# Range test of w1 as one minimum on VectorE, key and query bits' copies on ScalarE, in a fused hash-attention and Fourier-mixing kernel

## The chip, the cores and the metric

The kernel runs on one core of a Trainium2 chip. The metric is the device time of one execution in microseconds, as the median of several runs.

## The reference

The inputs are q, k and v of shape (4, 8, 768, 64), a projection of shape (64, 6), and two weight matrices that arrive as 64-bit floats. What is computed, cut to what matters:

```python
# attention: a query sees only the keys of its own hash bucket
q_bits = (einsum('bhsd,dk->bhsk', q, proj) > 0); k_bits = (same with k)
mask = bucket(q_bits)[..., :, None] == bucket(k_bits)[..., None, :]
scores = where(mask, (q @ k.T) / 8, -1e9)
attn = softmax(scores); x = attn @ v          # then heads side by side: (4, 768, 512)
# Fourier mixing and a two-layer network
u = x + real(fft2(x))
un = (u - mean(u)) / sqrt(var(u) + 1e-6)
out = u + relu(un @ w1) @ w2                  # w1 (512, 2048), w2 (2048, 512)
```

## The kernel before

The work goes by batch (4) and, inside a batch, by pair of heads (4), so there are 16 pairs, numbered 0 to 15. Each pair is handled in 6 chunks of 128 keys. For a chunk, TensorE makes the scores (L909), ScalarE takes their exp (L922, two halves, one for each half of the queries), VectorE adds the result to a running sum (L1043), and TensorE multiplies with v (L947). The bucket mask is, in pairs 0 to 4, a second product that is added to the scores in the same bank (L898): bits of the queries times bits of the keys, scaled so that a mismatch drives the exponent far down. From pair 5 the mask is a comparison on VectorE (L936).

The function `prepare(n + 1)` is a generator that is advanced once for each chunk of pair n. It transposes q and k of the next pair (L779 on VectorE), takes the squares' sums (L761 on ScalarE), makes the hash products (L812 on TensorE) and thresholds them (L816 on VectorE, reading the product's bank). For the query, two multiplications (L822) then make two masked copies of the bits; for the key, four copies (L828) put the bits at the partitions of the other half. These run after chunks 3 and 4. In pair 0 the key's copies alternate between VectorE and ScalarE (`evac`, L535 and L537).

During batch 0 a second generator, `weights1`, brings in w1. It is advanced in four of five chunks. Each of its 16 steps takes a block of 128x512 64-bit words that has been loaded into one of seven raw buffers, and `narrow` turns them into 32-bit floats: shifts and masks of the high words (L639, L643), a conversion of the low words on ScalarE (L647), an integer addition (L649). Then `narrow` tests the range: Abs of the high words (L654) and a Relu of `least` minus that with an accumulated sum (L655), whose sum is above zero where a magnitude was too small for a 32-bit float. The sum goes to a column of `strange`, which at the end, by a maximum (L1627), selects a slow path that is never taken with these inputs. `fetch` reloads the raw buffer (L704) when its last reader is done. After four steps the column means of w1 are made (`average`: ws at L664, part at L669, wm at L672) and subtracted (`centre`, L678). w2 passes through the same `narrow` later (its addition is L652).

At the end of a pair, `scale` normalises: key sums (L957), transposes and reciprocals (L979, L981, L982), small copies (L990), a transpose (L995) and a multiplication (L999). The last pair of a batch starts the Fourier stage's first folds (L1124 to L1142).

The buffers that matter here: the scores have two banks (`ps_sc`), and a chunk uses both, so scores of the next chunk start when the exp of the first half has read its bank. The exp's results have two buffers (`pks`), so the exp of chunk c+2 waits for the addition of chunk c to the running sum. `ps_1` has two banks for bits, ws and sums.

Batch 0 is written inside `manual_schedule`: each engine executes its instructions in the order in which the program issues them. One chunk's order is: scores and exp, addition to the sum, the previous pair's scaling, values of the previous chunk, a step of `prepare`, a step of `weights1`. From batch 1 on, a scheduler orders the engines.

Of the kernel before, what the change touches and what calls it, by code (L numbers as in the profile page):

```python
# [11 lines left out]
F32 = mybir.dt.float32  # L12
BF16 = mybir.dt.bfloat16
I32 = mybir.dt.int32
I64 = mybir.dt.int64
U32 = mybir.dt.uint32
AF = mybir.ActivationFunctionType
ALU = mybir.AluOpType
AX = mybir.AxisListType
# [5 lines left out]
DFF = 4 * DM  # L25
# [5 lines left out]
NDC = DM // P  # L31
GTT = 2
GT = GTT * P
WC = 512
# [451 lines left out]
def _main(  # L486
# [13 lines left out]
    nc = tc.nc  # L500
# [13 lines left out]
    def wt(shape, dtype, tag, name, bufs=2):  # L514
        return work.tile(shape, dtype, tag=tag, name=name, bufs=bufs)
# [78 lines left out]
    own = const.tile([P, 2], F32, tag="own", name="own")  # L594
# [25 lines left out]
    w2 = const.tile([P, NFC, DM], F32, tag="w2", name="w2")  # L620


    least = const.tile([P, 1], F32, tag="least", name="least")
    nc.gpsimd.memset(least, float(897 << 20))
    strange = const.tile([P, 2 * NDC * DFF // WC], F32, tag="strange", name="strange")
    nc.gpsimd.memset(strange, 0.0)

    def narrow(dst, raw, col, low=None):


        lo, hi = (raw[..., i] for i in range(2))
        t = lo.bitcast(F32)
        if low is None:

            low, t = lo, hi.bitcast(F32)
        di = dst.bitcast(I32)


        nc.vector.tensor_scalar(  # L639
            di, hi, 3, (1 << 30) - 1,  # L640
            op0=ALU.logical_shift_left, op1=ALU.bitwise_and,
        )
        nc.vector.scalar_tensor_tensor(  # L643
            di, hi, -(1 << 30), di, op0=ALU.bitwise_and, op1=ALU.bitwise_or
        )

        nc.scalar.activation(low, lo.bitcast(U32), AF.Copy, scale=2.0**-29)  # L647
        if len(di.shape) == 2:
            nc.vector.tensor_tensor(di, di, low, op=ALU.add)  # L649
        else:  # L650
            for i in range(di.shape[1]):
                nc.vector.tensor_tensor(di[:, i], di[:, i], low[:, i], op=ALU.add)  # L652

        nc.scalar.activation(t, hi, AF.Abs)  # L654
        nc.scalar.activation(  # L655
            t, t, AF.Relu, bias=least, scale=-1.0, accum_out=strange[:, col : col + 1]
        )
# [108 lines left out]
    def prepare(n):  # L766

        lite = n in LITE
        ts = {}
        for io, nm in enumerate("qk"):  # L770
            tn = nat.pop((nm, n))
            tt = wt([P, S], F32, nm + "t", f"{nm}t{n}")
            if n > 0:
                to, at = tt, tn
                if nm == "q":

                    to = tt.rearrange("p (i r n) -> p r i n", i=2, r=2)
                    at = tn.rearrange("p (r i n) -> p r i n", i=2, r=2)
                nc.vector.transpose(to, at)  # L779
            for g in range(2) if n == 0 else ():  # L780
                ps = pt([P, 3, P], f"tr{nm}{n}_{g}")
                for i in range(3):
                    c = 2 * i + g if nm == "q" else 3 * g + i
                    nc.tensor.transpose(ps[:, i, :], tn[:, c * P : (c + 1) * P], ident)
                if nm == "q":
                    for i in range(2):
                        dst = tt[:, i * HALF + g * HALF // 2 : i * HALF + (g + 1) * HALF // 2]
                        evac(
                            dst.rearrange("p (j c) -> p c j", c=3),
                            ps[:, :, i * D : (i + 1) * D],  # L790
                        )
                else:
                    evac(
                        tt[:, g * HALF : (g + 1) * HALF],
                        ps.rearrange("p c t -> p (c t)"),
                    )
            ts[nm] = tt
            yield
            norm(n, io, tn)
        if lite:  # L800

            qk = wt([P, 2, S], BF16, "qb", f"qkb{n}")
            qz = qk[:, 0].rearrange("p (g s) -> p g s", g=2)
            bits = {"q": qz[:, 0], "k": qk[:, 1, 0:HALF]}
            for io, nm in enumerate("qk"):
                ps = pt([P, HALF], f"bits{nm}{n}")
                for j in range(4):  # L810
                    h, g = divmod(j, 2)
                    nc.tensor.matmul(  # L812
                        ps[32 * j : 32 * j + 32, :], pjw[:, h * D : h * D + 32],
                        ts[nm][:, g * HALF : (g + 1) * HALF], start=True, stop=True,
                    )
                nc.vector.tensor_scalar(  # L816
                    bits[nm], ps, 0.0, off[:, io : io + 1],
                    op0=ALU.is_gt, op1=ALU.subtract,
                )
                if io == 0:  # L820
                    for g in (1, 0):
                        nc.vector.tensor_scalar(  # L822
                            qz[:, g], qz[:, 0], own[:, g : g + 1], None, op0=ALU.mult
                        )
                else:
                    for j in range(4):
                        to, at = (slice(32 * i, 32 * i + 32) for i in (j, j ^ 1))
                        (evac if n == 0 else nc.vector.tensor_copy)(  # L828
                            qk[to, 1, HALF:S], qk[at, 1, 0:HALF]
                        )  # L830
                yield
            preps[n] = ts["q"], ts["k"], qk, None
            return

        ps = pt([P, HALF], f"bits{n}")
        for j in range(4):
            src = ts["qk"[j // 2]][:, (j % 2) * HALF : (j % 2 + 1) * HALF]
            nc.tensor.matmul(  # L838
                ps[32 * j : 32 * j + 32, :], pj, src, start=True, stop=True
            )  # L840
        bt = wt([P, HALF], BF16, "bt", f"bt{n}")
        nc.vector.tensor_scalar(bt, ps, 0.0, None, op0=ALU.is_gt)
        yield

        qb = wt([P, 2, S], BF16, "qb", f"qb{n}")
        kb = wt([P, 2, NT], F32, "kb", f"kb{n}")
        for h in range(2):
            ps = ps_sc.tile([P, 2, 512], F32, tag="sc", name=f"qb{n}_{h}")
            for g in range(2):
                rows = slice(32 * g, 32 * g + 32)  # L850
                with behind() if g + h else nullcontext():
                    last[0] = nc.tensor.matmul(
                        ps[:, g, 0:HALF], pw[rows, h, :], bt[rows, :],
                        start=True, stop=True,
                    )
            evac(qb[:, h, :].rearrange("p (g s) -> p g s", g=2), ps[:, :, 0:HALF])
        ps = ps_sc.tile([P, 2, 512], F32, tag="sc", name=f"kb{n}")
        for c in range(NT):
            g, i = divmod(c, NT // 2)
            rows = slice(64 + 32 * g, 96 + 32 * g)  # L860
            with behind() if c else nullcontext():
                last[0] = nc.tensor.matmul(
                    ps[:, g, 2 * i : 2 * i + 2], bt[rows, i * P : (i + 1) * P],
                    pw[rows, :, 0], start=True, stop=True,
                )
        nc.vector.tensor_copy(
            kb.rearrange("p h (g i) -> p g i h", g=2),
            ps[:, :, 0:NT].rearrange("p g (i h) -> p g i h", h=2),
        )
        preps[n] = ts["q"], ts["k"], qb, kb  # L870
# [731 lines left out]
    for b in range(B):  # L1602
# [17 lines left out]
        if b == B - 1:  # L1620
            roomy[0] = True

            ms = const.tile([P, 3], F32, tag="ms", name="ms")
            nc.vector.tensor_reduce(ms[:, 0:2], norms, axis=AX.X, op=ALU.max)
            nc.vector.tensor_reduce(ms[:, 2:3], strange, axis=AX.X, op=ALU.max)  # L1627
            ps = pt([1, 3, P], "norms_t")
            for io in range(3):
                nc.tensor.transpose(ps[:, io, :], ms[:, io : io + 1], ident)  # L1630
            mt = const.tile([1, 5], F32, tag="mt", name="mt")
            nc.vector.tensor_reduce(mt[:, 0:3], ps, axis=AX.X, op=ALU.max)
            nc.vector.tensor_tensor(mt[:, 3:4], mt[:, 0:1], mt[:, 1:2], op=ALU.mult)
            nc.vector.tensor_scalar(
                mt[:, 4:5], mt[:, 3:4], (SAFE / SCALE / 2) ** 2, None, op0=ALU.is_gt
            )
            fl = const.tile([1, 1], I32, tag="fl", name="fl")
            nc.vector.scalar_tensor_tensor(
                fl, mt[:, 2:3], 0.0, mt[:, 4:5], op0=ALU.is_gt, op1=ALU.max
            )  # L1640
            large = nc.values_load(fl[0:1, 0:1], min_val=0, max_val=1)
# [54 lines left out]
```

## Time and profile before

| | before |
|---|---|
| median of 3 runs | 1077.52 us (1075.53 to 1077.93) |
| profiled execution | 1077.68 us, span 1075.9 us, TensorE clock 0.997 |
| TensorE busy | 1035.8 us, 96% |
| VectorE busy | 779.1 us, 72% |
| ScalarE busy | 500.7 us, 47% |
| L654, Abs of w1's and w2's blocks | 32 instructions, 0.69 us each |
| L655, Relu with sum | 32 instructions, 0.78 us each, and an accumulator read of 0.19 |
| L822, query bits' multiplications | 10 instructions, 0.32 us each |
| L828, key bits' copies | 16 instructions, 0.25 us each |

The profile is of one execution. An engine's busy time is the time in which an instruction of it was executing[...]. A line number is that of the kernel before, unless said otherwise; in the changed kernel the numbers are higher, by 1 up to `narrow` (640 for 639), by 7 after it (823 for 816), and by 10 in the last few functions.

### The profile page before, as it was taken

How to read it: one execution, taken by the hardware profiler on the slowest of the kernel's cores; microseconds unless marked ns; L12 is line 12 of the kernel's file. 1: busy time of each engine (PE TensorE's matmuls, PEld its weight loads, DVE VectorE, ACT ScalarE, POOL GpSimd, SP SyncE). 2: the span in 40 equal slices, each digit the busy share in tenths (PEclk: the TensorE clock that was granted, in tenths of full speed). 3: DMA queues.
4: the chain of work that ended last, by engine and by line, in shares of the span. 5: the costliest groups of instructions: out<-in, count | busy, mean ns of one | idle time of the engine just before them, and what ended most of it. 6: DMA issues, size and time to landing. Idle time of an engine off the chain costs nothing.

```text
span 1075.9 us, 14182 instructions
## 1 busy us (share of the span) xinstructions
PE 1035.8 (96%) x4965; PEld 633.6 (59%) x4965; DVE 779.1 (72%) x1326; ACT 500.7 (47%) x1057; POOL 59.1 (5%) x132
## 2 busy tenths in 40 slices
PE   7999899999999999999999999999999999999996
PEld 3333364447644585546664575655675579668575
DVE  5788969896799967877758877776856875644353
ACT  7888564762387324455336425354325522440420
POOL 0000000011000020010000020010000012200000
PEclk9999999999999999999999999999999999999999
DMA  8754551380154461224062232322032204222301
GB/s 206 201 140 86 104 141 46 124 238 6 32 142 158 139 195 24 56 62 87 12 198 71 66 116 98 55 64 65 16 119 91 65 25 171 65 74 98 118 20 42
DMA packets 175710, 103.13 MB, mean 96 GB/s; under 512 B 129552, under 2 KB 162960, under 8 KB 175632
## 3 DMA queue, kind: packets, MB, share of 16 engines
q1 hardware_dynamic: 169840, 88.65, 30.4%
q0 software_dynamic: 4224, 13.11, 3.8%
q8 instruction: 41, 0.67, 0.3%
q10 hardware_dynamic: 1568, 0.39, 0.2%
q14 instruction: 37, 0.30, 0.1%
HBM read 81.14 MB, written 20.97 MB: 95 GB/s over the span
## 4 chain that ended last, share of the span: by engine, by line
PE 77%; DVE 12%; ACT 6%; issue 2%; DMA 2%; SPq 2%; DVEq 0%; ACTq 0%
PE o L1352 26%; PE h_p L1473 22%; PE oo L947 10%; PE sc L909 9%; PE cs L1164 3%; DVE pk L936 2%; ACT pk L922 2%; PE A L1193 2%; DVE acc L1043 2%; PE B L1193 1%; DMA kn<-in_k_dram 1%; SPq L576 1%; PE sum L957 1%; DVE x L1207 1%; PE bits L838 1%
## 5 line engine op out<-in xcount | busy, mean ns | idle before, releaser
L1352 PE MATMUL o<-w,h 128*128 128x256 f32 x1152 | 259.4, 382 | 0.8 <-DVE w L1364 0.5
L1352 PEld LDWEIGHTS o<-w,h 128*128 128x128 f32 x1152 | 217.4, 191 | 42.0 <-issue 5.8
L922 ACT ACTIVATE pk<-sc 128x768 f32<-128x768 f32 x192 | 147.0, 808 | 77.1 <-PE oo L947 34.6
L1473 PE MATMUL h_p<-x,w 128*128 128x384 f32 x448 | 164.4, 494 | 3.1 <-ACT w L1540 1.7
L909 PE MATMUL sc<-qt,kt 64*128 64x384 f32 x768 | 154.6, 505 | 3.1 <-ACT pk L922 2.8
L936 DVE SCALAR_TENSOR_TENSOR pk<-qb,kb,pk 128x768 f32<-128x768 bf16 x132 | 128.7, 1011 | 38.2 <-ACT pk L922 38.1
L947 PE MATMUL oo<-pk,vn 128*64 128x385 f32 (+1 forms) x768 | 146.2, 495 | 0.8 <-DVE pk L936 0.6
L1473 PEld LDWEIGHTS h_p<-x,w 128*128 128x128 f32 x448 | 82.1, 190 | 69.0 <-issue 9.3
L1473 PE MATMUL h_p<-w 128*128 128x384 f32 x288 | 106.1, 490 | 0.1
L1043 DVE TENSOR_TENSOR acc<-acc,pk 128x1536 f32<-128x1536 f32 (+1 forms) x64 | 98.5, 1549 | 5.4 <-ACT pk L922 5.2
L947 PEld LDWEIGHTS oo<-pk,vn 128*64 128x64 f32 x768 | 50.5, 136 | 86.3 <-issue 73.1
L909 PEld LDWEIGHTS sc<-qt,kt 64*128 64x128 f32 x768 | 66.5, 187 | 57.2 <-issue 20.2
L1473 PEld LDWEIGHTS h_p<-w 128*128 128x128 f32 x288 | 53.6, 190 | 39.6 <-ACT w L1528 2.4
L1382 ACT COPY tq<-o 128x256 f32<-128x256 f32 x24 | 8.9, 372 | 104.3 <-PE o L1352 104.3
L1364 DVE SCALAR_TENSOR_TENSOR w<-o,rs,w 128x256 f32<-128x256 f32 x56 | 26.6, 479 | 41.2 <-PE o L1352 41.2
L1487 ACT ACTIVATE h<-h 128x384 f32<-128x384 f32 x72 | 37.4, 524 | 24.4 <-DVE h L1529 10.4
L1352 PE MATMUL o<-w 128*128 128x256 f32 x176 | 42.2, 383 | 0.2 <-DVE w L1364 0.2
L1524 DVE TENSOR_TENSOR h<-h 128x384 f32<-128x384 f32 x32 | 17.7, 554 | 29.6 <-ACT h L1523 29.6
L1102 POOL DMA_DIRECT2D out_dram<-w x30 | 16.3, 546 | 407.6 <-issue 314.6
L1352 PEld LDWEIGHTS o<-w 128*128 128x128 f32 x176 | 32.9, 190 | 7.5 <-DVE w L1364 1.2
L1371 ACT COPY tq<-o 128x256 f32<-128x256 f32 x24 | 8.8, 368 | 60.3 <-PE o L1352 60.2
L1398 DVE TENSOR_TENSOR tq<-tq,o 128x256 f32<-128x256 f32 x24 | 10.0, 417 | 36.4 <-PE o L1352 36.4
(171 smaller groups left out, 1316.9 us busy)
## 6 DMA issues: line engine op xcount, KB each, us to landing
w<-ad SPq DMA_DIRECT2D x168, 128.0 KB, 2.0
w<-bd SPq DMA_DIRECT2D x42, 512.0 KB, 4.4
zraw<-in_moe_w_ch_dram POOLq DMA_DIRECT2D x16, 512.0 KB, 3.9
bd<-w SPq DMA_DIRECT2D x14, 512.0 KB, 4.4
vn<-in_v_dram SPq DMA_DIRECT2D x32, 192.0 KB, 3.3
qn<-in_q_dram SPq DMA_DIRECT2D x120, 48.0 KB, 2.4
kn<-in_k_dram SPq DMA_DIRECT2D x60, 96.0 KB, 3.1
zraw<-in_moe_w_ch_dram SPq DMA_DIRECT2D x8, 512.0 KB, 7.1
```

The lines of the kernel that those rows point to most:

```text
L909: last[0] = nc.tensor.matmul(ps[:, h, 0:HALF], kt[rows, ks], qt[rows, qs], start=kb is not None or early, stop=not early,)
L922: done_by[ET.Activation] = nc.scalar.activation(pk[:, g, :, 0:HALF], ps[:, :, 0:HALF], AF.Exp, scale=SCALE)
L936: done_by[ET.DVE] = nc.vector.scalar_tensor_tensor(w, qb[:, h].rearrange("p (g s) -> p g s", g=2), kb[:, h, c : c + 1], w, op0=ALU.is_equa ...
L947: oo = nc.tensor.matmul(oos[g][h * D : (h + 1) * D, 0:w], nat["v", n][:, (2 * c + h) * D : (2 * c + h + 1) * D], pk[:, g, h, 0:w], start=( ...
L1043: done_by[ET.DVE] = nc.vector.tensor_tensor(acc[:, g], (first if c == 1 else acc)[:, g], new[:, g], op=ALU.add,)
L1164: nc.tensor.matmul(ps[:, pc + 2 * lo : pc + 2 * hi - 1 : 2], z[:, cp, pc, par, t * P : (t + 1) * P], ch[:, cp, pc, lo:hi], start=(cp == 0) ...
L1193: nc.tensor.matmul(ps[:, cols], F[:, par, k, t, j * P : (j + 1) * P], sq[:, t, k, cols], start=(t == 0), stop=(t == 1),)
L1352: nc.tensor.matmul(ps, a[:, r], right7[i][:, r], start=start and r == 0, stop=r == HF // 2 - 1, skip_group_check=not start,)
L1364: nc.vector.scalar_tensor_tensor(t[:, cols], src, r, t[:, cols], op0=ALU.mult, op1=ALU.add)
L1473: nc.tensor.matmul(ps, left[:, k], right[i][:, k], start=start and k == 0, stop=k == 1, skip_group_check=not start,)
L1487: done_by[ET.Activation] = nc.scalar.activation(h, h, AF.Relu)
L1524: done_by[ET.DVE] = nc.vector.tensor_tensor(c22, c21, c22, op=ALU.add)
```

## The change

The range test of w1's 16 blocks is a single reduction on VectorE: the minimum of the absolute values of the high words, read as 32-bit floats, into the column of `strange`. A comparison at the end turns these minima into flags. w2's blocks keep Abs and Relu on ScalarE, now also on the words read as floats. In pairs 0 to 4 the two multiplications of the query bits go from VectorE to ScalarE (a copy with a per-partition scale), and so do the four copies of the key bits in pairs 1 to 4.

```diff
-    nc.gpsimd.memset(least, float(897 << 20))
+    LEAST = float(np.int32(897 << 20).view(np.float32))
+    nc.gpsimd.memset(least, LEAST)
...
-        nc.scalar.activation(t, hi, AF.Abs)
+        if col < NDC * DFF // WC:
+            nc.vector.tensor_reduce(
+                strange[:, col : col + 1], hi.bitcast(F32), axis=AX.X,
+                op=ALU.min, apply_absolute_value=True,
+            )
+            return
+        nc.scalar.activation(t, hi.bitcast(F32), AF.Abs)
...
                     for g in (1, 0):
-                        nc.vector.tensor_scalar(
-                            qz[:, g], qz[:, 0], own[:, g : g + 1], None, op0=ALU.mult
+                        nc.scalar.activation(
+                            qz[:, g], qz[:, 0], AF.Copy, scale=own[:, g : g + 1]
                         )
...
-                        (evac if n == 0 else nc.vector.tensor_copy)(
+                        (evac if n == 0 else nc.scalar.copy)(
                             qk[to, 1, HALF:S], qk[at, 1, 0:HALF]
                         )
...
+            if moe_w_ch1.dtype == I64:
+                least_of = strange[:, 0 : NDC * DFF // WC]
+                nc.vector.tensor_scalar(least_of, least_of, LEAST, None, op0=ALU.is_lt)
             nc.vector.tensor_reduce(ms[:, 2:3], strange, axis=AX.X, op=ALU.max)
```

## The prediction

> **What bounds the kernel now.** I read the busy table first, then the order of the instructions, then the waits and the timeline of the stretch that the edit touches. Both programs issue the same instructions in the same order on PE, POOL and SP; on DVE and ACT they differ only up to the last key bits' copy of head pair 4, at 114 us. So the question is what happens from 10 to 120 us.
>
> ```profile
> PE 1035.8 (96%) x4965; PEld 633.6 (59%) x4965; DVE 779.1 (72%) x1326; ACT 500.7 (47%) x1057; POOL 59.1 (5%) x132
> ```
>
> Over the whole span TensorE is the bound. The same engines by stretches (us, then busy and count of PE, PEld, DVE, ACT, POOL; clock, DMA):
>
> ```profile
> 27.00:54.00 27.00, 24.64 (x170) 9.86 (x170) 21.60 (x38) 23.86 (x47) 0.00 (x0) 1.00 0.72 198
> 54.00:81.00 27.00, 24.53 (x169) 9.01 (x167) 23.80 (x41) 23.00 (x48) 0.00 (x0) 1.00 0.59 140
> 81.00:108.00 27.00, 27.00 (x194) 10.47 (x192) 24.19 (x44) 23.23 (x47) 0.11 (x1) 1.00 0.42 85
> ```
>
> Three engines are nearly full together. TensorE idles 2.4 of 27 us, then not at all. Its waits in 0 to 125 us (total, times, longest):
>
> ```profile
> PE sc L898 <- ACT pk L922: 5.3, 8, 1.5
> ...
> PE ws L664 <- DVE qkb L816: 1.3, 1, 1.3
> PE wm L672 <- ACT part L669: 1.1, 1, 1.1
> PE ws L664 <- DVE rt L979: 0.6, 1, 0.6
> ```
>
> Without the first load these are 8.3 us: all that a lighter ScalarE could give back. What matters is how late VectorE runs. The timeline of pair 0, chunks 2 to 4 (start, us, line):
>
> ```profile
> 24.23 0.85 PE L812 MATMUL bitsq<-qt,pjw 128*32 128x384 f32 x8
> ...
> 26.45 1.82 DVE L1043 TENSOR_TENSOR acc<-acc,pk 128x768 f32<-128x768 f32 x2
> ...
> 28.19 0.61 DVE L816 TENSOR_SCALAR qkb<-bitsq,off 128x384 bf16<-128x384 f32 x1
> ...
> 28.84 0.68 DVE L822 TENSOR_SCALAR qkb<-qkb,own 128x384 bf16<-128x384 bf16 x2
> ...
> 29.08 1.49 ACT L922 ACTIVATE pk<-sc 128x768 f32<-128x768 f32 x2
> ```
>
> The query bits of the next pair leave TensorE at 25.1 us; VectorE thresholds them (L816) only at 28.2, since it is behind. Nobody minds: pair 1's masks start at 34.7. In pair 1 the bits are out at 52.3 and thresholded at 57.4, and VectorE has no idle time from 44 to 62 us.
>
> [...] the trace has 510 for the 32x384 copy at L537. [...] the trace's exp pairs overlap by about 0.12. [...] starts on ACT follow its program order throughout.
>
> **The change, part by part.**
>
> ScalarE loses 16 x (L654 + L655) of 0.69 + 0.78 us with the accumulator read's 0.09 that shows: 1.55 from start to start, 24.8 us. It gains 10 multiplications (5 pairs x 2) of 0.60 and 16 copies of 0.42 to 0.51: about 13 us. VectorE gains 16 reductions of 0.61 (9.8 us) and one small compare (0.15), and loses 10 x 0.33 (L822) and 16 x 0.265 (L828), 7.5 us: net +2.4. These sums lie beside TensorE and decide nothing alone. The `least` constant, w2's casts (Abs keeps its shape) and the SP loads cost nothing: the same instructions, covered by the same work. The raw buffer is now released by the reduction instead of the Relu, so w1's fetches and the loads queued behind them on SP (q, k, v, and ch and sq once) go up to 8 us later in pair 2; by the trace's 2.2 to 3.2 us to landing, k of pair 3 arrives at about 83 us and its transpose comes at 87. q is close (about 81 against 82): bound 0 to +1 us, I take 0.
>
> **The added wait** is the expensive part. On ACT the two multiplications stand behind the square of k (L761) and *ahead of* L647 and of the exp of chunk 4; the copies stand ahead of the exp of chunk 5. They wait for VectorE's threshold, so exp, which feeds TensorE, now waits for VectorE's whole backlog. Queued behind the waiting multiplication: L647 (for which VectorE's L649 waits), the exp, then TensorE's scores of the next chunk, which need the bank that exp frees. Durations of the DVE steps are from start to start: transpose 0.90, convert 1.85, accumulate 1.74, threshold 0.63.
>
> *Start.* Before the first exp, L816's second threshold comes 0.65 us earlier, while the multiplications take 1.25 us on ScalarE instead of 0.68: exp starts 0.2 us earlier to 0.3 later, I take 0; the load below hides it.
>
> *Pair 0.* VectorE is free at about 18; the q load lands at about 19.0 (last issue 16.5 plus at least 2.2; VectorE took it at 19.2). From there: transpose, convert, reduction, accumulate, twice (10.2), threshold 0.63: it ends at 29.8 (28.8 before). Multiplications 1.25 (the second waits for the first), L647 0.70, first half of exp 0.81: scores of chunk 5 at 32.6 instead of 29.92, **+2.7**. After it the sequence is TensorE's as before.
>
> *Pair 1.* From L979 (39.46 before) to the end of the threshold VectorE works without a gap, 18.5 us; three reductions make 20.4. Before, scores of chunk 5 came 1.06 after the threshold (ws, L664, waited for it); now 1.25 + 0.81 + 0.05 = 2.1. **+2.9**, together 5.6.
>
> *Pair 2.* Copies, then L647, then exp hold L649, and one reduction more before the centring (64.16 before): +0.2, so it starts at 69.9. Up to the threshold: centring 2.4, three converts 5.7, three reductions 1.8, L979 to L982 1.0, three accumulates 5.2, L995 and L999 1.9, two transposes 1.8, threshold 0.6: 20.4, so 90.4. Multiplications 1.25, L647 0.70, half an exp 0.81: scores of chunk 5 at 93.2 instead of 84.13 (there TensorE set the pace and VectorE's lag was free): together 9.1. The threshold of k ends at 94.3; four copies 1.8, L647, half an exp: scores of pair 3 at 97.6 instead of 88.07, together **9.5**.
>
> *Pair 3.* VectorE needs 15.4 us from L979 to the threshold, with a reduction and the compare 16.2; it lies behind the first fold. It ends at 118.5; scores of chunk 5 at 120.6 instead of 106.89 (13.7). Behind the second fold, threshold of k at 122.4, copies, exp: the last values (L947) at 125.7 instead of 110.83, 14.9. There TensorE's waits for L979 (0.6) go, and rr and part come 14.0 later.
>
> Sum: **+14.0 us**. In pair 4 and later the orders agree again and the rest moves as a block. The profiled execution took 1077.68 (span 1075.9), the median is 1077.52: 1091.5.
>
> Bounds. About ten reductions lie on this path: at 0.36 each (the strided L639) -2.5, at 0.78 (L655's size) +1.7. Eight multiplications at 0.42 to 0.70: -1.5 to +0.8. Copies ±1, SP 0 to +1. That is +9 to +18.
>
> **Rivals.**
> - *Faster*: ScalarE was the bound and its relief reaches TensorE. One mechanism: exp of chunks 1 to 3 no longer stands behind Abs and Relu. For it: the 5.3 us above. It decides if the threshold ends before ScalarE gets to the multiplications, that is if VectorE is less than about 1 us behind. Then up to 8 us go: 1070 to 1076. Against: VectorE is 3 to 5 us behind and gets more work.
> - *Slower, but less*: VectorE catches up, because its own waits on ScalarE shrink (L649 on L647 3.4 us, one accumulate 1.7), and two of the four stalls vanish: +5, 1083.
> - *No change*: gain in pairs 0 and 1 (at most 6) against stalls in 2 and 3: 1077.5.
>
> **The numbers.** The stalls as worked out: 0.77, between 1086 and 1096. Less slow, 1079.7 to 1086: 0.11. Within 0.2% (2.2 us, about what a measurement of this kernel can tell from no change): 0.03. Faster: 0.09. The range 1082 to 1097 leaves out about 0.2.
>
> **What would show it.** After: TensorE waits of 2 us and more for exp at scores chunk 5 of pairs 0 to 3, ACT's idle time before the multiplications put down to L816 and some 12 us in all, ACT busy some 12 us less, DVE 2 more, reductions near 0.69 us, pair 4 starting near 130 us, the stretches after it unchanged. I am wrong if ACT does not idle before the multiplications, or if the reduction is far from 0.7.

## The result and the profile after

The changed kernel takes **1096.11 us** (median of 5 runs, 1095.03 to 1098.68) against 1077.20 for the kernel before on the same chip (1074.92 to 1077.93): ratio 1.0185, interval 1.0174 to 1.0197. It is slower, as forecast, by 18.9 us and not by 14.0. The profiled execution took 1095.03 us with a span of 1093.0, which is 17.1 more than the span before.

The busy table of the changed kernel (PE is TensorE, PEld its weight loads, DVE VectorE, ACT ScalarE, POOL GpSimd):

```profile
PE 1041.9 (95%) x4965; PEld 635.4 (58%) x4965; DVE 781.2 (71%) x1317; ACT 492.6 (45%) x1035; POOL 58.5 (5%) x132
```

ScalarE has 8.1 us less (the prediction had some 12) and VectorE 2.1 more. TensorE, with the same 4965 products, is busy for 6.1 us *more*. No part of the change adds a product, so products must run longer somewhere. The stretches say where (us, then busy and count of PE, PEld, DVE, ACT, POOL; granted clock, DMA share, GB/s):

```profile
27.00:54.00 27.00, 22.06 (x142) 8.50 (x134) 18.12 (x30) 18.59 (x37) 0.00 (x0) 0.94 0.63 177
54.00:81.00 27.00, 22.50 (x148) 8.16 (x148) 21.43 (x36) 16.88 (x34) 0.00 (x0) 0.94 0.47 134
81.00:108.00 27.00, 23.07 (x154) 8.84 (x152) 21.14 (x35) 18.51 (x36) 0.11 (x1) 0.94 0.50 95
108.00:135.00 27.00, 22.74 (x146) 7.96 (x142) 17.97 (x34) 15.26 (x34) 0.00 (x0) 0.87 0.48 104
```

Before, all three of the first stretches had clock 1.00 and no fewer than 169 products. Now there are about 150, no engine is full, and the clock is down to 0.94. The waits of 0 to 140 us (in us: total, times, longest):

```profile
ACT qkb L829 <- DVE qkb L823: 25.0, 5, 8.1
...
DVE w L650 <- ACT fraw L648: 15.9, 6, 5.7
PE sc L905 <- ACT pk L929: 13.3, 5, 4.4
...
PE ws L671 <- DVE qkb L823: 3.9, 1, 3.9
...
PE wm L679 <- ACT part L676: 1.1, 1, 1.1
```

The first line is the wait that the change adds: ScalarE's multiplications behind VectorE's threshold. The next two show whom it holds up: VectorE waits for the cast L648 that is queued behind it, and TensorE for exp (13.3 us in all). The timeline of pair 0, chunks 4 and 5, beside the one of before in the prediction:

```profile
22.79 0.85 PE L819 MATMUL bitsq<-qt,pjw 128*32 128x384 f32 x8
...
28.82 0.61 DVE L823 TENSOR_SCALAR qkb<-bitsq,off 128x384 bf16<-128x384 f32 x1
...
29.47 1.26 ACT L829 ACTIVATE qkb<-qkb,own 128x384 bf16<-128x384 bf16 x2 [5.11 <-DVE qkb L823]
30.63 0.64 ACT L648 ACTIVATE fraw<-fraw 128x512 int32<-128x512 uint32 x1
31.18 1.49 ACT L929 ACTIVATE pk<-sc 128x768 f32<-128x768 f32 x2
...
32.02 0.34 PE L905 MATMUL sc<-qkb 64*128 64x384 bf16 x2 [4.44 <-ACT pk L929]
...
33.16 2.07 ACT L835 COPY qkb<-qkb 32x384 bf16<-32x384 bf16 x4 [0.49 <-DVE qkb L823]
```

The chain is the predicted one, link by link: ScalarE stands idle for 5.11 us, then come the two multiplications, L648, half an exp, and the scores of chunk 5 start. The query bits had been ready since 23.6. What the prediction did not have is the state in which TensorE comes out of such a wait. Pair 2, chunk 5, TensorE alone:

```profile
93.93 0.51 PE L905 MATMUL sc<-qkb 64*128 64x384 bf16 x2 [3.92 <-ACT pk L929]
94.20 1.51 PE L916 MATMUL sc<-qt,kt 64*128 64x384 f32 x4
```

The same two lines of the kernel before took 0.34 and 0.81 us:

```profile
84.13 0.34 PE L898 MATMUL sc<-qkb 64*128 64x384 bf16 x2
84.30 0.81 PE L909 MATMUL sc<-qt,kt 64*128 64x384 f32 x4
```

The window of the changed kernel over these products gives the reason. The granted clock stands in the column ahead of the last two:

```profile
94.00:96.00 2.00, 2.00 (x10) 1.26 (x11) 1.97 (x4) 1.51 (x3) 0.00 (x0) 0.50 0.00 0
```

TensorE is busy for all of the 2 us, at half clock (0.50).

### The profile page after: what moved, and what is told of

The parts are those of the page before. It is cut to its first block, busy times and chain, and to the rows that moved or that the text cites. A ratio compares the mean times of both kernels' runs of the same rounds, so it can differ in the third digit from the quotient of the medians.

```text
span 1093.0 us, 14146 instructions
## 1 busy us (share of the span) xinstructions
PE 1041.9 (95%) x4965; PEld 635.4 (58%) x4965; DVE 781.2 (71%) x1317; ACT 492.6 (45%) x1035; POOL 58.5 (5%) x132
## 4 chain that ended last, share of the span: by engine, by line
PE 75%; DVE 14%; ACT 5%; DMA 2%; issue 2%; SPq 2%; ACTq 0%; DVEq 0%
PE o L1359 26%; PE h_p L1480 22%; PE oo L954 9%; PE sc L916 9%; PE cs L1171 2%; DVE acc L1050 2%; DVE pk L943 2%; PE A L1200 2%; ACT pk L929 2%; PE B L1200 1%; SPq L576 1%; PE sum L964 1%; DVE x L1214 1%; PE bits L845 1%; DMA kn<-in_k_dram 1%
## 5 line engine op out<-in xcount | busy, mean ns | idle before, releaser
L929 ACT ACTIVATE pk<-sc 128x768 f32<-128x768 f32 x192 | 148.1, 809 | 82.8 <-PE oo L954 34.2
L916 PE MATMUL sc<-qt,kt 64*128 64x384 f32 x768 | 158.3, 515 | 3.1 <-ACT pk L929 2.8
```

What stands on the lines that cost most here:

```text
L916: last[0] = nc.tensor.matmul(ps[:, h, 0:HALF], kt[rows, ks], qt[rows, qs], start=kb is not None or early, stop=not early,)
L929: done_by[ET.Activation] = nc.scalar.activation(pk[:, g, :, 0:HALF], ps[:, :, 0:HALF], AF.Exp, scale=SCALE)
```

## Experiments

My theory: two costs, the order of ScalarE's queue (multiplications and copies that wait for VectorE hold back exp: above, L648 and L929 start at 30.63 and 31.18, behind L829 at 29.47), and the half clock that follows a long wait of TensorE (0.50 behind 3.92 us in pair 2). Rivals: the work itself (the reductions on VectorE, the copies on ScalarE), or a low clock that has another cause.

**One part alone.** e1_test_only: the changed kernel with the bits' operations back on VectorE (each call is shown on one line).

```diff
-    nc.scalar.activation(qz[:, g], qz[:, 0], AF.Copy, scale=own[:, g : g + 1])
+    nc.vector.tensor_scalar(qz[:, g], qz[:, 0], own[:, g : g + 1], None, op0=ALU.mult)
...
-    (evac if n == 0 else nc.scalar.copy)(
+    (evac if n == 0 else nc.vector.tensor_copy)(
```

> The change with only the range test moved to VectorE; multiplications and copies of the bits stay on VectorE. Theory (what costs is that exp stands behind the bits' multiplications and copies on ScalarE, and these behind VectorE's backlog): no exp waits for a threshold, no TensorE wait above 2.5 us, TensorE's clock stays at 1.00, ScalarE is 25 us lighter. VectorE's 16 reductions of 0.60 us only delay ws, centring and the bits of the next pair: +0 to +3 us, 1077 to 1080. Rival (VectorE is the bound, the reductions cost most of it): +10 us, 1087 or more.

Measured: 1082.44, ratio 1.0059 (1.0042 to 1.0076). More than expected. The timeline of TensorE shows a wait that I had taken for harmless:

```profile
59.19 1.93 PE L671 MATMUL ws<-w,ones 128*32 128x512 f32 x8 [3.87 <-DVE qkb L823]
```

The average's product ws comes behind the key bits' product and waits for the threshold. Before it waited 1.28 us there; with the reductions ahead of the threshold it waits 3.87, and then takes 1.93 instead of 1.07: half clock here too (0.50 from 58 to 64 us).

e2_mults_only and e3_copies_only: the kernel before, with one of the two moves (shown in the same way).

```diff
-    nc.vector.tensor_scalar(qz[:, g], qz[:, 0], own[:, g : g + 1], None, op0=ALU.mult)
+    nc.scalar.activation(qz[:, g], qz[:, 0], AF.Copy, scale=own[:, g : g + 1])
```

and, in the other kernel:

```diff
-    (evac if n == 0 else nc.vector.tensor_copy)(
+    (evac if n == 0 else nc.scalar.copy)(
```

> The kernel before with only the query bits' multiplications moved to ScalarE. Theory: exp of chunk 4 in pairs 0 to 3 waits for the query threshold, then for L647, Abs and Relu, which are queued behind the multiplications: TensorE waits of 3 to 4 us at scores of chunk 5, clock 0.5 after them; +10 to +14 us, 1087 to 1091. Rival (reductions): within 2 us of before.

> The kernel before with only the key bits' copies moved to ScalarE. Theory: exp of chunk 5 waits for the key threshold and 2.07 us of copies. By the timeline of before that costs 0 in pair 0, 1 us in pair 1, 3 in pair 2 and 5 in pair 3 (behind the second fold), with the clock lowered after the last: +8 to +11 us, 1085 to 1088. Rival (reductions): within 2 us of before.

Measured: 1092.48 (ratio 1.0151, 1.0134 to 1.0168) and 1089.35 (1.0127, 1.0109 to 1.0145), both a little above what was expected. Their waits in 0 to 140 us, the multiplications alone:

```profile
PE sc L898 <- ACT pk L922: 16.2, 11, 4.0
ACT qkb L822 <- DVE qkb L816: 15.9, 5, 6.2
```

and the copies alone:

```profile
ACT qkb L828 <- DVE qkb L816: 11.7, 4, 5.4
...
PE sc L898 <- ACT pk L922: 10.7, 11, 2.9
PE oo L947 <- ACT pk L922: 4.7, 1, 4.7
```

Each move by itself puts ScalarE behind VectorE, and TensorE waits 15 to 16 us for exp (5.8 in the kernel before). The three parts' losses (0.6, 1.5 and 1.3%) add up to 3.4%, the whole costs 1.85%. They share waits, so they don't add: with both moves together, in the next kernel, TensorE waits 17.9 us for exp and not twice as long.

**Undo the range test.** e7_no_test_move is the kernel before with both moves of e2 and e3 together.

> The change without its range test: test as before on ScalarE, multiplications and copies on ScalarE as in the change. Theory (the two moves of the key and query bits make the loss, and the range test's move gives ScalarE 3 us per pair back but lays a reduction ahead of the threshold): ScalarE now has 3 us more per pair than in the change and the threshold comes some 1.2 us earlier per pair; the waits of TensorE for exponentials add up to 20 us or more and the time is 1097 to 1104, the slowest of all. Rival (the reductions on VectorE ahead of the threshold make the loss): below 1090, near to the multiplications alone (1092.5) at most.

Measured: 1095.99, ratio 1.0188 (1.0171 to 1.0205). My number was too high, and the rival's too low: it is the changed kernel's own loss. With both moves made, the range test's place makes no measurable difference.

**Keep TensorE busy.** e4_warm is the changed kernel with the key bits' product of pairs 1 to 4 made five times over, which lies in the wait.

```diff
-                for j in range(4):
+                for j in [*range(4)] * (5 if io and n else 1):
```

> The whole change, with the key bits' product of pairs 1 to 4 made five times over the same bank (the last counts), so that TensorE works through 3.1 of the 4 us for which it waits before scores of chunk 5. Theory with the clock (the stalls of 4 us cost 14 us by themselves, and the granted clock of 0.5 for some 3 us after each the other 3.4): scores of chunk 5 take 1.7 us instead of 2.9 to 3.3, clock 0.997, 3 to 4 us faster than the change, 1092 to 1093. Rival (the slow matmuls are not from the idle time): no gain, 1096, or slower by the added products.

Measured: 1089.71, ratio 1.0130 (1.0113 to 1.0147). The profile counts 40 product instructions in the place of 8 in each of the four pairs, and the kernel is *faster* than the changed one, by 6.4 us between the medians, or by 5.6 when each is compared with the kernel before that was measured beside it (18.9 and 13.3 us slower). ScalarE waits for the threshold as long as there (26.9 us), and the scores of chunk 5 of pair 0 start as late (31.95 against 32.02), but at full clock (1.00 from 32 to 34 us, where the changed kernel has 0.62):

```profile
31.95 0.34 PE L905 MATMUL sc<-qkb 64*128 64x384 bf16 x2 [1.47 <-ACT pk L929]
32.11 0.82 PE L916 MATMUL sc<-qt,kt 64*128 64x384 f32 x4
```

So the half clock is a separate cost. Its size is best read at wm, where the changed kernel is 17.4 us behind the kernel before and e4 13.9: 3.5 us, as much as I had expected. The rest of e4's gain lies after the change's stretch and says nothing on it. Some 0.7 us come where e4 has its products in another order (128 to 137 us). Another 1.6 us come near 390 us: there the changed kernel has a stretch at clock 0.50 (390.86 to 394.28), as the kernel before has one (373.00 to 376.42), and e4's execution has none (its mean clock is 0.997, as in the kernel before). In pair 1 the half clock is still there (clock 0.51 and 0.64 from 64 to 68 us): behind the filler ws waits 1.29 us, and the scores wait again.

**Waits without the change.** e6_ladder is the kernel before with additional squares on ScalarE.

```diff
             accum_out=norms[:, io, n : n + 1],
         )
+        if io == 1:
+            for _ in range({1: 2, 2: 4, 3: 6, 4: 8}.get(n, 0)):
+                nc.scalar.activation(junk, tn, AF.Square)
```

> The kernel before with 2, 4, 6 and 8 additional squares of k (0.84 us each) on ScalarE in the stretches of pairs 0, 1, 2 and 3: waits of TensorE of growing length, with none of the change's operations. The squares' results go where the kernel's own square of k goes, unused. Theory (a long enough wait of TensorE halves its clock for about 3 us afterwards, whatever caused it): the shortest waits (to about 2 us) leave the clock at 0.9 or above, those above about 4 us are followed by a window of 2 us at about 0.50, in which four f32 scores products take 1.5 us instead of 0.81; the length between is where the change's own waits lie. Rival (the low clock comes with the change's operations, or is a throttle of the chip that happened to fall there): no stretch of low clock behind any wait. Time 1084 to 1098 by the sum of the waits.

Measured: 1090.88 in its one run. TensorE's waits for exp above 1.5 us:

```profile
30.82 0.34 PE L901 MATMUL sc<-qkb 64*128 64x384 bf16 x2 [2.13 <-ACT pk L925]
...
50.88 0.34 PE L901 MATMUL sc<-qkb 64*128 64x384 bf16 x2 [1.56 <-ACT pk L925]
...
90.59 0.51 PE L901 MATMUL sc<-qkb 64*128 64x384 bf16 x2 [3.86 <-ACT pk L925]
...
118.21 0.50 PE L901 MATMUL sc<-qkb 64*128 64x384 bf16 x2 [3.33 <-ACT pk L925]
```

None of the change's operations is here, and waits of 3.86 and 3.33 us are followed by half clock (0.50 from 90.5 to 92.5 and from 118.2 to 120.2 us): the change's operations are not needed for it. But one expectation failed. Behind the wait of 2.13 us the first products are fast, and a moment later they are not:

```profile
30.00:32.00 2.00, 1.18 (x10) 0.92 (x11) 1.79 (x5) 1.63 (x4) 0.00 (x0) 1.00 0.95 348
32.00:34.00 2.00, 2.00 (x8) 0.53 (x6) 1.63 (x4) 1.47 (x2) 0.00 (x0) 0.53 0.69 270
```

Before this, from 28 to 32 us, TensorE had been busy for 1.87 of 4 us. The length of one wait thus does not decide alone; the last section has more such cases.

**Behind the exp.** e5_defer is the changed kernel with the multiplications issued behind the exp of chunk 4 and the copies behind the exp of chunk 5; the `yield` goes from the end of the loop's body to ahead of them.

```diff
+                yield
                 if io == 0:
                     for g in (1, 0):
                         nc.scalar.activation(
...
-                yield
             preps[n] = ts["q"], ts["k"], qk, None
```

> The whole change, with the multiplications issued one step later (behind the exponentials of chunk 4 instead of ahead of them) and the copies one step later too. Nothing is left out. Theory (the loss is the in-order queue of ScalarE: the multiplications wait there for VectorE's threshold and hold back exponentials that TensorE waits for, and the 4 us waits then halve TensorE's clock): the wait of the multiplications for the threshold falls from 25 us to under 5 in the first 140 us, no wait of TensorE for exponentials is above 2.5 us, the clock is back at about 0.99 in each stretch; the time is 1078 to 1083, near to the range test alone (1082.4). Rival (the loss is work: ScalarE's 3 us more per pair, VectorE's reductions): the time stays at 1090 or above, since the same instructions run on the same engines.

Measured: 1080.90, ratio 1.0046 (1.0029 to 1.0062): three quarters of the loss is gone with the same instructions on the same engines. ScalarE in pair 0:

```profile
26.42 1.50 ACT L929 ACTIVATE pk<-sc 128x768 f32<-128x768 f32 x2
29.78 1.26 ACT L830 ACTIVATE qkb<-qkb,own 128x384 bf16<-128x384 bf16 x2 [1.85 <-DVE qkb L823]
30.95 1.49 ACT L929 ACTIVATE pk<-sc 128x768 f32<-128x768 f32 x2
```

The exp of chunk 4 starts at 26.42 where the changed kernel had it at 31.18. The multiplications still wait for the threshold, 12.9 us in all and not "under 5" as I wrote, but no exp stands behind them that TensorE needs soon: the scores wait 1.0 us for exp in all. One stretch, 54 to 81 us, is not back at full clock (0.87): ws still waits 3.87 us there, as in e1.

e9_defer_mults has the multiplications deferred in the same way, and the copies on VectorE.

> The range test on VectorE as in the change, the copies left on VectorE, and the multiplications on ScalarE but issued behind the exponentials of chunk 4. Nothing is left out. Theory: no exponential stands behind a wait for the threshold; VectorE has the 1.25 us of the multiplications less ahead of the copies than in the range test alone; TensorE's waits at the average's product stay; the time is 1078 to 1083. Rival (any move of these operations onto ScalarE's queue costs several us): 1088 or above.

Measured: 1081.86, ratio 1.0057 (1.0041 to 1.0074), as expected; not to be told from e5 or e1.

**The wait of ws.** Three kernels issue ws one step of the weights' work later: e5, e1 and the kernel before with

```diff
             if half:
-                centre(half[0], next(half[1]))
-                half = None
+                avg = next(half[1])
+                if avg is not None:
+                    centre(half[0], avg)
+                    half = None
...
                     half = f, average(f)
-                    next(half[1])
```

> The deferred version (multiplications and copies on ScalarE behind the exponentials, range test on VectorE), with the average's product ws issued one step of the weights' work later, so that in pair 1 it stands behind the scores of chunk 5 and not between the key bits' product and them. Nothing is left out. Theory (what is left of the loss there is the 3.87 us wait of ws for the threshold at 59 us and the 6 us of half clock that go with it): no wait of ws above 1.5 us in the first 140 us, clock at 0.98 or above in every stretch of 27 us, and the time 4 to 6 us below the deferred version: 1074 to 1078. Rival (what is left is VectorE's and ScalarE's work): 1080 to 1082, as the deferred version.

> The range test alone on VectorE (multiplications and copies on VectorE as in the kernel before), with the same later ws. Nothing is left out. Theory: the range test by itself costs its 5 us only through the wait of ws and the half clock behind it; without it 1074 to 1079, against 1082.4 for the range test alone. Rival: VectorE, with the reductions ahead of the thresholds and the copies behind them, lets the scores of chunk 5 wait in the place of ws: 1080 or above.

> The kernel before with the same later ws: control for the two others. Its waits of ws are 1.3 us and its clock is full, so by the theory at most 1 us comes off: 1075 to 1078, within 0.2% of the kernel before. Rival (ws's place costs by itself, whatever waits there): 3 us or more below the kernel before.

Measured: e10 1079.72 (ratio 1.0032, 1.0020 to 1.0044), e11 1078.96 (1.0023, 1.0012 to 1.0034), e12 1075.25 (0.9989, 0.9980 to 0.9997). In e10 and e11 ws waits at most 0.4 us in pair 1. e11 is 0.36% below e1, and their intervals do not touch. But e12, without the change, gains 0.1% by the same step, so it is the measure for e11: against it the range test costs 0.34% (1.0023 over 0.9989), where e1 has 0.59% against the kernel before. The wait of ws and its half clock are thus a part of the range test's loss, less than half of it by these figures. The rest I have not taken apart; e11 still has half clock behind waits of ws at 114 and 116 us (0.36 and 1.49 us; clock 0.67 from 116 to 118 and 0.50 from 118 to 120 us). e10 misses its expectation by 1.7 us, lies next to the rival's 1080 to 1082, and is not to be told from e5: the later ws did not help it measurably. It has three small waits in a row (0.85 us for exp, 0.77 and 0.72 for the deferred copies, from 61 to 65) and half clock behind them (0.64 and 0.51 from 64 to 68 us).

## Why the prediction was right and where it was wrong

The starts of TensorE's work tell it step by step (us; line L898 before, L905 after):

| Scores | before | predicted | after | late, predicted | late, measured |
|---|---|---|---|---|---|
| pair 0, chunk 4 | 25.50 | as before | 23.57 | 0 | -1.9 |
| pair 0, chunk 5 | 29.92 | 32.6 | 32.02 | 2.7 | 2.1 |
| pair 1, chunk 0 | 34.73 | as at chunk 5 | 38.47 | 2.7 | 3.7 |
| pair 1, chunk 5 | 59.05 | 64.6 | 65.55 | 5.6 | 6.5 |
| pair 2, chunk 5 | 84.13 | 93.2 | 93.93 | 9.1 | 9.8 |
| pair 3, chunk 0 | 88.07 | 97.6 | 99.49 | 9.5 | 11.4 |
| pair 3, chunk 5 | 106.89 | 120.6 | 122.28 | 13.7 | 15.4 |
| wm (L672, now L679) | 118.35 | | 135.74 | 14.0 | 17.4 |

- **Sign and mechanism: right.** ScalarE idles before the multiplications, put down to the threshold; exp and L648 stand behind them; TensorE waits 4.44, 3.92 and 3.90 us for exp at chunk 5 of pairs 0, 2 and 3. In pair 1 it is ws, standing ahead of the scores, that waits (3.87). The idle time on ScalarE is 25 us, not "some 12": it reaches the multiplications 5 to 8 us ahead of the threshold. That costs nothing by itself; what counts is when the threshold ends. After wm nothing more is lost: 17.4 there, 17.1 in the span.
- **Durations: right but for one.** The reduction takes 0.68 us and 0.60 from start to start, as estimated from L678 of the kernel before (the same 128x512, 0.68 us, four in 2.48). The two multiplications take 1.26 against 1.25; the 0.60 for one was an estimate of mine with no trace behind it (0.61 measured). The four copies take 2.07 against 1.8, an estimate in which they overlap: at 0.51 each they don't. ScalarE's busy time falls by 8.1 us and not by 12, as it gets 14.2 us of new work (8.1 for the copies, 6.1 for the multiplications) and gives up 22.3, not 24.8. The copies hold up exp as predicted, but behind the half clock it does not show: in the changed kernel the first scores of pairs 1 to 3, which follow them, start without a wait. In e4, at full clock, the first scores of pair 3 and the last values of pair 3 wait 0.65 us each for exp.
- **VectorE's path: right.** In pair 1 I had 20.4 us from L979 to the end of the threshold. It is L986 now, from 43.20 to 63.50: 20.3. Only its start is late, 43.20 where 39.46 + 2.7 had been expected: the pair before had lost 0.6 us less than predicted at chunk 5, and then 1.6 at half clock.
- **The step that failed was a term missing from the sum**: products were costed at the durations of before, whatever wait stood ahead of them. From chunk 5 of a pair to the next pair's start (in pair 3 to wm) the prediction lets the lag grow by 0.7 us in all, for the copies. Measured, it grows by 1.6 in pair 0, 0.5 in pair 1 (6.5 to 7.0 at 71.05), 1.6 in pair 2 and 2.0 in pair 3: 5.8 us. The same stretches in e4, at full clock (1.00), have 0.0 in pair 0, 0.7 in pair 2 and 0.0 in pair 3. The difference, with the 0.5 of pair 1, is what the half clock cost: about 5.0 us, where the prediction had nothing. In pair 1 ws takes 1.94 for 1.07 us, but that is not on the path: in e4, where ws runs at full clock (1.00 from 62 to 64 us), the scores start as long after it (1.99 us in both).
- **The waits were a little over-sized.** Without the half clock the lag at wm is about 12.4 us (17.4 less 5.0), where the prediction has 14.0: pair 0 has 2.1 for 2.7, pair 2 2.8 for 3.5, pair 3 4.0 for 4.2. The two errors have opposite signs, and part of the missing term was hidden by this. That e4 comes out at 13.3 us by the medians, near to 14.0, is in part luck: it holds 1.65 us of half clock in pair 1, and has none near 390 us.
- **A smaller term**: *Start* was taken as 0. In fact the relief of ScalarE brings the scores of chunk 4 of pair 0 forward by 1.9 us, and the wait at chunk 5 grows by as much, as VectorE sets its end. What it changes in the sum is 0.6 (2.1 for 2.7).
- **The rivals.** The "slower, but less" case did not come: no stall vanished. The gain of "faster" is real, but it is 1.9 us in pair 0 and is lost in the wait that follows.
- Of the 18.9 us between the medians the profile shows 17.4; the changed kernel's profiled execution is the fastest of its five, the rest is not traced. Their mean clocks are 0.985 to 0.987 against 0.988 in the profiled one, so more half clock is likely there.

The traces show the missing term. In the changed kernel the clock is at 0.50 from 32.47 to 35.88, 63.19 to 66.60, 93.91 to 97.32 and 121.21 to 128.04 us, around the ends of the waits of 4.44, 3.87, 3.92 and 3.90 us (32.02, 63.56, 93.93 and 122.28), and TensorE is at work for 3.41, 2.99, 3.39 and 5.76 us of these stretches. The waits of 3.48 and 4.04 us in e2, 4.75 in e3 and 3.45 in e7 are followed by products at half clock too (0.61 from 34 to 36, 0.50 and 0.50 from 122 to 124 and 0.57 from 34 to 36 us). A wait of such a length is not needed, though, as the 2.13 us wait above shows.

## What to carry to other kernels

An operation moved to an idle engine takes its wait along: look at what is queued behind it there, and issue it behind the work that others need, not ahead. When a step of the prediction makes TensorE wait as long as here (3.87 to 4.44 us, with a clock of 0.50 behind it), add what the products lose at half clock, here 0.5 to 2.0 us for each wait. An engine's idle share says nothing on this: ScalarE, at 47% before, got less work and the kernel got slower.

## What the runs showed of the hardware that I had not expected

A wait is not needed in one piece. In e10 three waits of 0.85, 0.77 and 0.72 us (TensorE busy for 2.16 of the 4 us from 60 to 64) were followed by a clock of 0.64 and 0.51 from 64 to 68 us.

Nor did waits of one length always end alike. In e3 a wait of 2.00 us that ended at 48.98 (busy 1.99 from 46 to 50) was followed by a clock of 0.50 from 50 to 52 us; behind one of 2.01 us that ended at 78.65 (busy 1.99 from 76 to 80) the clock stayed at 1.00. In e6, 2.13 us (busy 1.87 from 28 to 32) were followed by 0.53. In e3, 2.90 us that ended at 93.46 were followed by 0.55 from 94 to 96 us; in e2, 2.98 us that ended at 94.51 were followed by 1.00. So neither the length of a wait of 2 to 3 us nor the busy time of these 4 us tells whether half clock follows; what does, these figures do not show. Near 390 us no wait is long: in the changed kernel the longest in the 4 us ahead of the stretch is 1.59 us (busy 2.14 from 386.86 to 390.86), and the clock goes to 0.50; the kernel before had the same busy time (2.14 from 369 to 373) and the same clock behind it, and e4 has no such stretch. Two executions can thus differ by a stretch that the change has nothing to do with.
